# Sums and turns one to a slot at a block change, two stored pieces a step, x loaded in parts, the last block turned by TensorE, and a conversion that starts 6 half iterations later

## The chip, the cores and the metric

The kernel runs on one core of one Trainium2 chip. The metric is the device time of one execution in microseconds (us): 1709.61 us, the median of three runs (1707.02 to 1710.48). The profiled execution took 1710.2 us; its span, from the first instruction to the last, is 1708.4 us.

## The reference

Three layers follow one another, in float64 inputs and with a float32 result:

```python
p_packed = softmax_attention(p, k, v)          # 8 batches x 8 heads, 576 tokens, 32 packed queries, head 64
attn     = softmax_attention(q, p_packed, p_packed)
x        = attn as 4608 tokens x 512
h = x @ w_in                                   # 512 -> 2048
g = max(h, 0) + alpha * min(h, 0)
x = g @ w_out                                  # 2048 -> 512
g = x @ w_gate;  val = x @ w_val               # 512 -> 1536 each
out = (g / (1 + exp(-g)) * val) @ w_out2       # 1536 -> 512, returned as float32
```

## The kernel before, in words

All matmuls of the two large layers split their operands into a high and a low part and do three products for one (`mm3`: low weights by high x, high by high, high weights by low x).

The program has two phases. The first, 256 iterations, makes attention and the first large layer. Beside it, in half iterations (slots) from `GROUP0 = 84` on, DVE, ACT and POOL convert the weights of the last layer (`more_weights2`): each raw piece of 64-bit words becomes float32, is combined into seven forms, split in two and stored to device memory (`wgvd`, `wo2d`).

The second phase is the last layer, with a seven-product scheme for 2x2 blocks (forms A11, S2, A12, S3, S1, A22, S4). It goes over 6 blocks of 768 tokens and, in each, over 12 slices of the 1536 columns: 72 calls of `gv_step`, here called steps 0 to 71. One step does on PE seven products of six matmuls, into one bank of tag `h` (tiles xb, then vb) and one of tag `at` (yb). Each product but the first into a bank must wait until DVE or ACT has read what the product before left there: `u2 = yb + p1`, `u3 = yb + p1`, `u3 = vb + u3`, `p1 = yb + p1`, `u2 = vb + u2` on DVE (function `add`), p1 and the Silu on ACT. Between the products, at six places (`between(0)` to `between(5)`, called slots in this phase), stand the units of the output product of the step pair before: three matmuls each, seven units a step, so 63 matmuls a step.

The output of a block is summed in tiles `sums` (totals A12, S1, S2, A22, S4, each in two halves e = 0, 1) and in four banks o_acc that keep A11 and S3 over the whole block. When the last step pair of a block is done, which falls into the first two steps of the next block (steps 12 and 13, 24 and 25, ...), the totals are added to each other by `more`, turned by DVE's transpose into `os` or `osA` tiles by `put`, and stored by `store`, in four DMAs of 48 KB to a piece, eight pieces to a block. This is called a block change; there are five, and the sixth block ends the program in `out_last`.

SP's queue issues all loads: two tiles gv of a step's weights (`load_gv`, 896 KB each, two steps ahead, so that the buffers of step n take the weights of step n + 2), tiles wp of the output weights (`load_wo2`), and 16 DMAs a block that load the x of the next block into eight tiles xr (`load_x`). It also issues the stores, which `store` places behind the newest gv load.

The order of the work on each engine is set by a scheduler when the program is built; `tc.issue_after(ins)` keeps what is written in its block behind `ins` on the engine of `ins`. A wait on an engine holds everything behind it on that engine.

Of the kernel before, what the change touches and what calls it, by code (L numbers as in the profile page):

```python
# [108 lines left out]
def tile_kernel(  # L111
# [1031 lines left out]

    raw2, xs2, gvw, wo2 = {}, {}, {}, {}

    def load_x(s):
        for t in range(2):
            for c in range(KC):
# [62 lines left out]
    def prepare_x(s, name):  # L1211
        if name == "load":
            load_x(s)
        elif name == "S":
            sums_x(s)
        elif name == "D4":
            last_sum(s)
        else:
            split_x(s, name)
# [36 lines left out]
    def product(bank, n, k, start):  # L1256
# [14 lines left out]
                )  # L1271
        before[:] = [last]

    def add(out, bank, x):
        return nc.vector.tensor_tensor(out=out, in0=bank, in1=x, op=ALU.add)  # L1275

    def gv_step(n, between):

        s, f = divmod(n, NF2)
        p1, u2, u3, s1, s2 = (
            gp2.tile([P, T], F32, tag=t, name=f"{t}_{n}", bufs=b)
            for t, b in (("p1", 1), ("u2", 1), ("u3", 1), ("s1", 3), ("s2", 3))
        )
        def bank(tag, name):
            return ps.tile([P, 512], F32, tag=tag, name=f"{name}{n}", bufs=2)[:, :T]

# [36 lines left out]
        load_gv(n + 2)  # L1325
        store(n, 2)
# [11 lines left out]
    def form(m, name, x):  # L1338

        hi = gp2.tile([P, T], F32R, tag="fh", name=f"fh{m}_{name}", bufs=5)  # L1340
        nc.scalar.activation(out=hi, in_=x, func=AF.Copy)  # L1341
        lo = gp2.tile([P, T], F32R, tag="fl", name=f"fl{m}_{name}", bufs=5)
        by_dve = m == PAIRS - 1 and name in ("S2", "S4")
        (nc.vector if by_dve else nc.gpsimd).tensor_tensor(out=lo, in0=x, in1=f32(hi), op=ALU.subtract)  # L1344
        forms[m, name] = hi, lo

    def combine(out, x, y, op, last):
        engine = nc.vector if last else nc.gpsimd
# [21 lines left out]
    def forms_last(m):  # L1370

        last = m == PAIRS - 1
        a12, a22 = both[2 * m + 1]
        s2 = both[2 * m][0]
        form(m, "A22", a22)
        combine(a12, a12, s2, ALU.subtract, last)
        form(m, "S4", a12)

    banks, sums = {}, {}

# [14 lines left out]
                    sums[n, k] = tiles[j][:, c * T : (c + 1) * T]  # L1395
        return sums[name, e]

    def put(s, name, e, at_slot):

        t, dh = dict(A12=(0, 0), S4=(0, 1), A22=(1, 0), S1=(1, 1))[name]  # L1400
        if s == NBLK - 1:
            o = utile("u", [P, T], f"os{name}{e}_{s}")
        elif name == "A22":
# [6 lines left out]
        stores.append((at_slot, o, (2 * s + t) * T, 256 * dh + P * e))  # L1410
        if s == NBLK - 1:
            store(NBLK * NF2 + 9, 0)

    def store(n, i):

        for job in [j for j in stores if j[0] <= (n, i)]:
            stores.remove(job)
            at_slot, o, r0, c0 = job
            with tc.issue_after(newest[-1].ins) if n < NBLK * NF2 else ExitStack():
                for a in range(4):  # L1420
                    c = c0 + 32 * a
                    queue = nc.scalar if a % 2 and n > NBLK * NF2 else nc.sync
                    queue.dma_start(
                        out=out[r0 : r0 + T, c : c + 32].rearrange("(b j) i -> j b i", j=32),
                        in_=o[32 * a : 32 * a + 32].rearrange("p (b i) -> p b i", i=32),
                    )

    def more(to, e, x, engine=nc.vector):
        engine.tensor_tensor(out=total(to, e), in0=x, in1=total(to, e), op=ALU.add)  # L1429
# [9 lines left out]
            )  # L1439
        done(last)  # L1440

    def out_unit(m, i, at_slot):

        k, e = divmod(i, 2)
        name = OUT_FORMS[k]
# [11 lines left out]
        if first:  # L1457
            nc.scalar.activation(out=total(name, e), in_=bank, func=AF.Copy)
        else:
            more(name, e, bank)  # L1460
        if not last:
            return
        if name == "S1":
            more("S4", e, total("S1", e))
            more("S1", e, banks[f"acc{2 + e}"])
        elif name == "S2":
            u2 = total("S2", e)
            more("S1", e, u2)
            put(s, "S1", e, at_slot)
            more("A22", e, u2)  # L1470
            more("S4", e, u2, nc.gpsimd)
        else:
            put(s, name, e, at_slot)

    LAST = (
        ("A12", "A12"), ("S1", "S1"), ("S1", "S4"), ("S2", "S1"), ("S2", "A22"), ("A22", "A22"),
        ("S2", "S4"), ("S4", "S4"),
    )

    def out_last():  # L1480

        m = PAIRS - 1
        forms_later(m)
        forms_last(m)
        for e in range(2):
            more("S4", e, total("S1", e))
            more("S1", e, banks[f"acc{2 + e}"])
            for to in "S1", "A22", "S4":
                more(to, e, total("S2", e))
        at_end = {}  # L1490
        for tag, to in ("", "A12"), ("free", "S1"), ("acc0", "S4"), ("acc2", "A22"):
            for e in range(2):
                if tag == "free":
                    name = ("h", "at")[e]
                    at_end[to, e] = ps.tile([P, 512], F32, tag=name, name=f"oe{e}", bufs=2)[:, :T]
                else:
                    at_end[to, e] = banks[f"acc{int(tag[3:]) + e}" if tag else ("h", "at")[e]]
        for i, (name, to) in enumerate(LAST):
            start = to not in [t for _, t in LAST[:i]]
            stop = to not in [t for _, t in LAST[i + 1 :]]  # L1500
            for e in range(2):
                unit(at_end[to, e], m, OUT_FORMS.index(name), e, start, stop)
                if stop:
                    more(to, e, at_end[to, e])
                    put(NBLK - 1, to, e, (0, 0))

    due_at, after_at = {}, {}
    for m in range(PAIRS):
# [10 lines left out]
    def out_next(n, i):  # L1519

        for job in due_at.pop((n, i), ()):
            out_unit(*job, (n, i))
        if (n, i) in after_at:
            after_at.pop((n, i))()


    def steps(it, late):
# [27 lines left out]
    assert kinds[0] is None  # L1555
    gp1.close()
    gp2 = ctx.enter_context(tc.tile_pool(name="g2", bufs=1))
    for n in range(NBLK * NF2):
        gv_step(n, lambda i, n=n: out_next(n, i))
    assert not due_at and not after_at  # L1560
# [38 lines left out]
```

## Time and profile before

| | |
|---|---|
| median of three runs | 1709.61 us |
| profiled execution, its span | 1710.2 us, 1708.4 us |
| granted TensorE clock, mean | 0.968 |
| PE busy | 1590.0 us (93%), 10943 matmuls |
| DVE, POOL, ACT busy | 1098.1 us (64%), 1012.0 us (59%), 739.6 us (43%) |
| bytes moved by DMA | 330.74 MB |

Busy time is the sum over an engine's instructions; a clock of 1 is the higher of two levels, 2.4 GHz, and 0.5 the lower, 1.2 GHz. In rows of the timeline the first number is the start in us from the span's start, the second the time; `x4` are four instructions in a row, and the brackets hold the idle time of the engine before the row and what ended it. Matmuls are pipelined: one is listed with some 0.33 us, and the next starts 0.17 us after it.

### The profile page before, as it was taken

Reading aid. Unit: us, or ns where it says so; the run is one execution under the profiler, and the core shown is the slowest. Engines: PE = TensorE matmul, PEld = TensorE weight load, DVE = VectorE, ACT = ScalarE, POOL = GpSimd, SP = SyncE. Lnnn points to the kernel's source line nnn. Section 1 sums busy time; section 2 is a strip of 40 time slices with the busy share of each in tenths; the row PEclk is TensorE's granted clock in tenths of the full one; section 3 lists DMA queues with packets and bytes.
Section 4 is the critical chain, followed back from the end, with each engine's and each line's share of the span. In section 5 each row is a group of like instructions: output and inputs, shape, how many; then the busy total and the mean of one; then the engine's idle time right before and its main releaser. Section 6 shows DMA issues by size and latency. Waiting matters only on the chain.

```text
span 1708.4 us, 30336 instructions
## 1 busy us (share of the span) xinstructions
PE 1590.0 (93%) x10943; PEld 1493.3 (87%) x10943; DVE 1098.1 (64%) x1898; ACT 739.6 (43%) x1666; POOL 1012.0 (59%) x1063
## 2 busy tenths in 40 slices
PE   7598999989999999999999899989988998998897
PEld 4367798879898888989999899979988988998896
DVE  6868667575667676763356836845774683677357
ACT  6575654555555555555333333332322333233221
POOL 4748656666766767674456546655654664556552
PEclk8799999999999999999999999989999998999998
DMA  9414365646565555544666776776766687666762
GB/s 282 134 49 132 95 186 147 179 105 168 137 166 128 165 142 152 147 164 128 228 229 249 255 251 253 277 220 234 279 223 231 245 298 223 222 241 208 258 247 64
DMA packets 304231, 330.74 MB, mean 194 GB/s; under 512 B 206016, under 2 KB 257232, under 8 KB 299472
## 3 DMA queue, kind: packets, MB, share of 16 engines
q1 hardware_dynamic: 297680, 328.01, 59.9%
q8 instruction: 86, 1.41, 0.3%
q10 hardware_dynamic: 6400, 0.79, 0.3%
q14 instruction: 65, 0.53, 0.1%
HBM read 274.47 MB, written 54.26 MB: 192 GB/s over the span
## 4 chain that ended last, share of the span: by engine, by line
PE 70%; DVE 11%; DMA 6%; issue 4%; POOL 4%; ACT 2%; SPq 1%; DVEq 0%; POOLq 0%; ACTq 0%
PE acc L1115 6%; PE acc L1121 5%; PE acc L1116 5%; PE yb L326 4%; PE yb L328 4%; PE yb L327 4%; PE h L326 3%; DMA gv<-wgvd 3%; PE xb L326 3%; PE h L328 3%; PE h L327 3%; DVE sums L1429 3%; PE vb L326 3%; PE vb L327 3%; PE vb L328 3%
## 5 line engine op out<-in xcount | busy, mean ns | idle before, releaser
L1102 POOL TENSOR_TENSOR lo<-g,hi 128x288 fp32r<-128x288 f32 x256 | 233.1, 912 | 227.4 <-ACT hi L1100 187.3
L1092 DVE SCALAR_TENSOR_TENSOR g<-h,sg,m 128x288 f32<-128x288 f32 x256 | 130.6, 511 | 184.5 <-ACT m L1089 166.9
L1319 POOL TENSOR_TENSOR s<-s,u 128x384 f32<-128x384 f32 x72 | 73.0, 1013 | 256.3 <-ACT s L1312 256.3
L1275 DVE TENSOR_TENSOR u<-yb,p 128x384 f32<-128x384 f32 x144 | 80.0, 556 | 201.3 <-PE yb L328 185.6
L326 PE MATMUL h<-a2h,ppw 128*128 128x288 f32 x512 | 160.6, 314 | 31.7 <-DVE g L1092 22.6
L1349 POOL TENSOR_TENSOR s<-s,s 128x384 f32<-128x384 f32 x141 | 150.5, 1067 | 46.0 <-DVE s L1316 40.5
L1100 ACT ACTIVATE hi<-g 128x288 fp32r<-128x288 f32 x256 | 113.0, 442 | 144.8 <-DVE g L1092 141.7
L326 PE MATMUL yb<-ring,gv 128*128 128x384 f32 x432 | 149.9, 347 | 21.7 <-DVE u L1275 21.7
L1344 POOL TENSOR_TENSOR fl_S<-s,fh_S 128x384 fp32r<-128x384 f32 x142 | 145.4, 1032 | 25.4 <-ACT fh_S L1341 25.1
L1089 ACT ACTIVATE m<-h,sal 128x288 f32<-128x288 f32 x256 | 126.3, 495 | 66.3 <-PE h L328 65.4
L328 PE MATMUL h<-a2l,ppw 128*128 128x288 f32 x512 | 152.5, 299 | 2.2 <-POOL a2l L562 2.1
L326 PEld LDWEIGHTS h<-a2h,ppw 128*128 128x128 f32 x512 | 97.3, 190 | 63.8 <-DVE g L1092 33.2
L327 PE MATMUL h<-a2h,ppw 128*128 128x288 f32 x512 | 152.2, 297 | 0.0
L327 PE MATMUL yb<-ring,gv 128*128 128x384 f32 x432 | 147.8, 342 | 0.0
L328 PE MATMUL yb<-ring,gv 128*128 128x384 f32 x432 | 147.7, 342 | 0.0
L1275 DVE TENSOR_TENSOR u<-vb,u 128x384 f32<-128x384 f32 x144 | 79.9, 555 | 92.3 <-PE vb L328 92.3
L1312 ACT ACTIVATE s<-p 128x384 f32<-128x384 f32 x72 | 37.8, 525 | 213.4 <-DVE p L1275 213.4
L1344 POOL TENSOR_TENSOR fl_A<-s,fh_A 128x384 fp32r<-128x384 f32 x108 | 112.5, 1042 | 27.1 <-ACT fh_A L1341 26.0
L326 PE MATMUL xb<-ring,gv 128*128 128x384 f32 x288 | 101.1, 351 | 25.9 <-DMA gv<-wgvd 21.9
L326 PEld LDWEIGHTS yb<-ring,gv 128*128 128x128 f32 x432 | 83.7, 194 | 26.1 <-DVE u L1275 26.1
L985 POOL TENSOR_TENSOR cva<-cva,cva 128x256 fp32r<-128x256 f32 x126 | 96.9, 778 | 10.2 <-ACT cva L984 9.6
L328 PEld LDWEIGHTS h<-a2l,ppw 128*128 128x128 f32 x512 | 97.4, 191 | 4.6 <-POOL a2l L562 3.8
(297 smaller groups left out, 5027.8 us busy)
## 6 DMA issues: line engine op xcount, KB each, us to landing
gv<-wgvd SPq DMA_DIRECT2D x144, 896.0 KB, 8.0
wp<-wo2d SPq DMA_DIRECT2D x36, 1024.0 KB, 5.1
wp<-wo2d SPq DMA_DIRECT2D x36, 768.0 KB, 4.4
wgvd<-cva SPq DMA_DIRECT2D x84, 256.0 KB, 2.8
wo2d<-cva SPq DMA_DIRECT2D x42, 256.0 KB, 2.6
v<-in_v_dram SPq DMA_DIRECT2D x16, 576.0 KB, 4.8
cva<-in_moe_w_in_dram SPq DMA_DIRECT2D x7, 1024.0 KB, 8.8
kr<-in_k_dram SPq DMA_DIRECT2D x96, 72.0 KB, 2.7
```

Of the source, the lines that this page charges most:

```text
L326: nc.tensor.matmul(o, wlo, xhi, start=start, stop=False, **kw)
L327: nc.tensor.matmul(o, whi, xhi, start=False, stop=False, **kw)
L328: return nc.tensor.matmul(o, whi, xlo, start=False, stop=stop, **kw)
L985: nc.gpsimd.tensor_tensor(out=lo, in0=full, in1=f32(hi), op=ALU.subtract)
L1089: begun[it] = marks[f"u{it}"] = nc.scalar.activation(out=m, in_=hp, func=AF.Copy, scale=sal[:, f : f + 1])
L1092: made[it] = marks[f"m{it}"] = nc.vector.scalar_tensor_tensor(out=g32, in0=hp, scalar=sg[:, f : f + 1], in1=m, op0=ALU.mult, op1=ALU.max)
L1100: rounded[n] = nc.scalar.activation(out=hi, in_=x, func=AF.Copy)
L1102: nc.gpsimd.tensor_tensor(out=lo, in0=x, in1=f32(hi), op=ALU.subtract)
L1115: nc.tensor.matmul(acc[dc], lo[:, f % WP, c], ghi, start=start, stop=False)
L1275: return nc.vector.tensor_tensor(out=out, in0=bank, in1=x, op=ALU.add)
L1344: (nc.vector if by_dve else nc.gpsimd).tensor_tensor(out=lo, in0=x, in1=f32(hi), op=ALU.subtract)
L1349: engine.tensor_tensor(out=out, in0=x, in1=y, op=op)
```

## The change

- `NEXT_X`: the x of the next block is no longer loaded by one call at slice 3, but by four calls at slices 2 to 5 (x00, x10, x12, x02), two tiles each.
- `later`, `do_later`: at a block change, the additions of totals to each other and the turns are put into a list, `jobs2`, and `out_next` takes one of them at each slot, behind the newest `add`. The two additions S4 += S2 stay on POOL at once.
- `store` stores two pieces at the end of a step, whatever is ready.
- `sums_ahead`, `out_last`: in the last block S4 += S1 goes to POOL at step 71; the other additions of totals stand behind `forms_last`. The totals are turned by PE (three 128x128 transposes against `ident` to a piece), copied by ACT and stored in one DMA a piece, where before DVE turned them and four DMAs on SP and ACT stored a piece.
- `GROUP0`: 90 for 84.

```diff
-GROUP0 = 84
+GROUP0 = 90
-NEXT_X = dict(load=3, A11=6, S=6, S2=7, A12=8, D4=9)
+NEXT_X = dict(x00=2, x10=3, x12=4, x02=5, A11=6, S=6, S2=7, A12=8, D4=9)
...
     def add(out, bank, x):
-        return nc.vector.tensor_tensor(out=out, in0=bank, in1=x, op=ALU.add)
+        ins = nc.vector.tensor_tensor(out=out, in0=bank, in1=x, op=ALU.add)
+        ahead[:] = [ins]
+        return ins
...
+    def store():
+        for _ in range(min(len(stores), 2)):
+            o, r0, c0 = stores.pop(0)
+            with tc.issue_after(newest[-1].ins):
...
+    def do_later():
+        if jobs2:
+            with tc.issue_after(ahead[-1].ins):
+                jobs2.pop(0)[2]()
...
-        if name == "S1":
-            more("S4", e, total("S1", e))
-            more("S1", e, banks[f"acc{2 + e}"])
+        if name == "A12":
+            wait.append(("A12", e, lambda: put(s, "A12", e)))
+        elif name == "S1":
+            later("S1", e, lambda: more("S4", e, total("S1", e)))
+            later("S1", e, lambda: more("S1", e, banks[f"acc{2 + e}"]))
...
         elif name == "S2":
-            u2 = total("S2", e)
-            more("S1", e, u2)
-            put(s, "S1", e, at_slot)
-            more("A22", e, u2)
-            more("S4", e, u2, nc.gpsimd)
+            more("S4", e, total("S2", e), nc.gpsimd)
+            if e:
+                for i in range(2):
+                    later("S2", i, lambda i=i: more("S1", i, total("S2", i)))
...
+    LAST = """
+        A12-A12 S1-S1 S1-S4 combined >A120 >A121 S2-S1 S2-A22 A22-A22 >S10 >S11 S2-S4 S4-S4
+        >A220 >A221 >S40 >S41
+    """
...
+                for g in range(T // P):
+                    c = slice(g * P, (g + 1) * P)
+                    last = nc.tensor.transpose(bank[:, c], total(to, e)[:, c], ident)
...
+            nc.scalar.activation(out=o, in_=bank, func=AF.Copy)
+            nc.sync.dma_start(
```

DVE at the first block change, from the read of vb that ends step 12 to the first read of yb in step 13 (u2_13), before:

```order
L1275 TENSOR_TENSOR u2_12_12090<-vb12_12152,u2_12_12090 128x384
L1429 TENSOR_TENSOR sums0_10977<-o_acc2_10922,sums0_10977 128x384
L1429 TENSOR_TENSOR sums0_10977<-o_h_10973,sums0_10977 128x384
L1429 TENSOR_TENSOR sums0_10977<-o_acc3_10951,sums0_10977 128x384
L1429 TENSOR_TENSOR sums1_10978<-o_at_10989,sums1_10978 128x384
L1316 TENSOR_TENSOR s1_12_12092<-s1_12_12092,u2_12_12090 128x384
L1429 TENSOR_TENSOR sums0_10977<-sums0_10977 128x384
L1429 TENSOR_TENSOR sums1_10978<-sums0_10977,sums1_10978 128x384
L1429 TENSOR_TENSOR sums0_10977<-sums1_10978,sums0_10977 128x384
L1429 TENSOR_TENSOR sums1_10978<-sums1_10978 128x384
L1275 TENSOR_TENSOR u2_13_12230<-yb13_12235,p1_13_12229 128x384
```

The same stretch now, and on to the second read of yb (u3_13):

```order
L1279 TENSOR_TENSOR u2_12_12090<-vb12_12149,u2_12_12090 128x384
L1444 TENSOR_TENSOR sums0_10977<-o_acc2_10922,sums0_10977 128x384
L1444 TENSOR_TENSOR sums0_10977<-o_h_10973,sums0_10977 128x384
L1322 TENSOR_TENSOR s1_12_12092<-s1_12_12092,u2_12_12090 128x384
L1444 TENSOR_TENSOR sums1_10978<-o_at_10989,sums1_10978 128x384
L1279 TENSOR_TENSOR u2_13_12212<-yb13_12217,p1_13_12211 128x384
L1444 TENSOR_TENSOR sums1_10978<-o_h_10973,sums1_10978 128x384
L1444 TENSOR_TENSOR sums1_10978<-sums0_10977,sums1_10978 128x384
L1444 TENSOR_TENSOR sums0_10977<-o_acc3_10951,sums0_10977 128x384
L1279 TENSOR_TENSOR u3_13_12213<-yb13_12217,p1_13_12211 128x384
```

The four additions of totals to totals have left the place ahead of u2_13; one of them stands behind it, and three follow in the rest of step 13 and in step 14.

SP at the first block change, from the gv load that step 13 issues for step 15 to the next but one, before (gv15 belongs to step 15; os and osA are stores):

```order
L1236 DMA gv15_0_12332<-wgvd3_484 128x1792
L1236 DMA gv15_1_12333<-wgvd3_484 128x1792
L1423 DMA out_0_dram<-os_12136 32x12x32 x8
L1423 DMA out_0_dram<-osA220_0_12254 32x12x32 x4
L1423 DMA out_0_dram<-osA221_0_12274 32x12x32 x4
L1423 DMA out_0_dram<-os_12136 32x12x32 x4
L1245 DMA wp8_0_12438<-wo2d2_495 128x2048
L1236 DMA gv16_0_12468<-wgvd4_485 128x1792
L1236 DMA gv16_1_12469<-wgvd4_485 128x1792
L1423 DMA out_0_dram<-os_12136 32x12x32 x4
```

The same stretch now:

```order
L1238 DMA gv15_0_12315<-wgvd3_484 128x1792
L1238 DMA gv15_1_12316<-wgvd3_484 128x1792
L1429 DMA out_0_dram<-os_12255 32x12x32 x8
L1247 DMA wp8_0_12412<-wo2d2_495 128x2048
L1238 DMA gv16_0_12447<-wgvd4_485 128x1792
L1238 DMA gv16_1_12448<-wgvd4_485 128x1792
L1429 DMA out_0_dram<-os_12255 32x12x32 x8
L1247 DMA wp8_1_12532<-wo2d2_495 128x1536
L1238 DMA gv17_0_12563<-wgvd5_486 128x1792
```

Twenty stores stood between two steps' gv loads, and now eight do, as they do behind the gv loads of the two steps that follow.

SP in steps 10 and 11, where the x of block 2 is loaded, now (before, the same sixteen DMAs stood at the same two places, with tiles 02 and 03 ahead of 10 to 13):

```order
L1155 DMA xr2_00_12459<-x1d5_80 128x192
L1155 DMA xr2_00_12459<-x1d6_81 128x192
L1155 DMA xr2_01_12462<-x1d5_80 128x192
L1155 DMA xr2_01_12462<-x1d6_81 128x192
L1247 DMA wp6_0_11933<-wo2d0_493 128x2048
L1238 DMA gv12_0_11963<-wgvd0_481 128x1792
L1238 DMA gv12_1_11964<-wgvd0_481 128x1792
L1155 DMA xr2_10_12575<-x1d6_81 128x96
L1155 DMA xr2_10_12575<-x1d7_82 128x288
L1155 DMA xr2_11_12578<-x1d6_81 128x96
```

The scheduler places the four calls of slices 2 to 5 of block 1 into steps 10 and 11, around the same gv load as before.

## Rows read from the trace of the kernel before

**Rows 1.** Waits of PE: who waited for whom, us in total, times, longest
```profile
PE xb L326 <- DMA gv<-wgvd: 21.9, 5, 5.2
PE yb L326 <- DVE u L1275: 21.7, 10, 4.1
```

**Rows 2.** Timeline of PE at the first block change, steps 13 and 16
```profile
961.79 0.44 PE L326 MATMUL xb<-ring,gv 128*128 128x384 f32 x1 [0.50 <-DVE u L1275]
...
965.38 0.34 PE L328 MATMUL xb<-ring,gv 128*128 128x384 f32 x1
969.79 0.44 PE L326 MATMUL yb<-ring,gv 128*128 128x384 f32 x1 [4.08 <-DVE u L1275]
...
1004.46 0.66 PE L326 MATMUL xb<-ring,gv 128*128 128x384 f32 x1 [3.59 <-DMA gv<-wgvd]
```

**Rows 3.** Stretches: length, busy us (x) of PE, PEld, DVE, ACT, POOL, clock, DMA share
```profile
961.80:1017.00 55.20, 47.53 (x252) 46.92 (x253) 28.64 (x47) 16.72 (x36) 29.28 (x28) 0.94 0.71 225
1107.00:1163.60 56.60, 48.53 (x253) 47.92 (x254) 28.76 (x47) 16.72 (x36) 29.27 (x28) 0.91 0.68 220
1253.60:1312.30 58.70, 49.78 (x252) 49.17 (x253) 28.65 (x47) 16.72 (x36) 29.25 (x28) 0.88 0.67 212
1402.40:1459.90 57.50, 48.23 (x253) 47.62 (x254) 28.65 (x47) 16.72 (x36) 29.27 (x28) 0.91 0.68 216
1549.90:1607.10 57.20, 48.87 (x252) 48.25 (x253) 28.66 (x47) 16.71 (x36) 29.28 (x28) 0.91 0.69 217
1618.10:1672.90 54.80, 54.80 (x316) 54.80 (x316) 29.82 (x55) 16.16 (x34) 34.51 (x35) 1.00 0.67 243
```

**Rows 4.** Timeline of DVE at the first block change
```profile
959.71 1.56 DVE L1429 TENSOR_TENSOR sums<-sums,sums 128x384 f32<-128x384 f32 x2
961.19 0.55 DVE L1275 TENSOR_TENSOR u<-vb,u 128x384 f32<-128x384 f32 x1
...
964.10 1.37 DVE L1429 TENSOR_TENSOR sums<-sums 128x384 f32<-128x384 f32 x1
965.39 2.62 DVE L1429 TENSOR_TENSOR sums<-sums,sums 128x384 f32<-128x384 f32 x2
967.93 1.34 DVE L1429 TENSOR_TENSOR sums<-sums 128x384 f32<-128x384 f32 x1
969.19 0.55 DVE L1275 TENSOR_TENSOR u<-yb,p 128x384 f32<-128x384 f32 x1
```

**Rows 5.** Timeline of POOL beside these
```profile
965.01 1.31 POOL L1349 TENSOR_TENSOR s<-s,s 128x384 f32<-128x384 f32 x1
```

**Rows 6.** Timeline of SP's queue, steps 12 to 15; the time is that of the issue
```profile
959.92 0.79 SPq L1236 DMA_DIRECT2D gv<-wgvd  x2
...
978.48 9.15 SPq L1423 DMA_DIRECT2D out_dram<-os  x8
987.73 4.00 SPq L1423 DMA_DIRECT2D out_dram<-osA  x8
...
994.38 1.81 SPq L1236 DMA_DIRECT2D gv<-wgvd  x2
```

**Rows 7.** The page's DMA issues: count, KB each, us from issue to landing
```profile
gv<-wgvd SPq DMA_DIRECT2D x144, 896.0 KB, 8.0
```

**Rows 8.** Timeline at the end: PE, DVE, and SP's last stores
```profile
1687.92 0.69 PE L326 MATMUL o_h<-fh_A,wp 128*128 128x384 f32 x1 [3.33 <-ACT fh_A L1341]
...
1684.91 1.94 DVE L1429 TENSOR_TENSOR sums<-o_acc,sums 128x384 f32<-128x384 f32 x4
...
1701.15 1.01 DVE L1409 STREAM_TRANSPOSE osS<-sums 128x384 f32<-128x384 f32 x2
...
1702.87 2.14 SPq L1423 DMA_DIRECT2D out_dram<-osS  x4
```

**Rows 9.** One line's instructions: the phase-one transposes by PE, ns min/median/max
```profile
L704 PE MATMUL et<-ident,E x72: 270/272/275, 218.1 to 684.7; 128*96 128x128 f32 x72
```

**Rows 10.** Timeline of PE in iteration 233 of phase one
```profile
762.91 0.40 PE L326 MATMUL h<-a2h,ppw 128*128 128x288 f32 x1 [2.34 <-DVE g L1092]
```

More of the change, by code (lines that the diff above doesn't have):

```diff
@@ L1144, in tile_kernel, with load_x @@
     raw2, xs2, gvw, wo2 = {}, {}, {}, {}
-    def load_x(s):
-        for t in range(2):
-            for c in range(KC):
+    def load_x(s, ts=range(2), cs=range(KC)):
+        for t in ts:
+            for c in cs:
                 raw = utile("u", [P, T], f"xr{s}_{t}{c}")
@@ L1213, in prepare_x @@
             load_x(s)
+        elif name[0] == "x":
+            load_x(s, (int(name[1]),), range(int(name[2]), int(name[2]) + 2))
         elif name == "S":
@@ L1325, in gv_step @@
         load_gv(n + 2)
-        store(n, 2)
+        store()
         if s + 1 < NBLK:
@@ L1343, in form @@
         by_dve = m == PAIRS - 1 and name in ("S2", "S4")
-        (nc.vector if by_dve else nc.gpsimd).tensor_tensor(out=lo, in0=x, in1=f32(hi), op=ALU.subtract)
         forms[m, name] = hi, lo
+        return (nc.vector if by_dve else nc.gpsimd).tensor_tensor(
+            out=lo, in0=x, in1=f32(hi), op=ALU.subtract
+        )
     def combine(out, x, y, op, last):
@@ L1396, in total, with place, put @@
         return sums[name, e]
-    def put(s, name, e, at_slot):
+    def place(s, name, e):
         t, dh = dict(A12=(0, 0), S4=(0, 1), A22=(1, 0), S1=(1, 1))[name]
-        if s == NBLK - 1:
-            o = utile("u", [P, T], f"os{name}{e}_{s}")
-        elif name == "A22":
+        return (2 * s + t) * T, 256 * dh + P * e
+    def put(s, name, e):
+        if name == "A22":
             o = utile("x", [P, T], f"os{name}{e}_{s}")
@@ L1409, in put @@
         nc.vector.transpose(out=o, in_=total(name, e))
[L1410 to L1419, printed above, removed]
+        stores.append((o, *place(s, name, e)))
+    def store():
+        for _ in range(min(len(stores), 2)):
+            o, r0, c0 = stores.pop(0)
+            with tc.issue_after(newest[-1].ins):
                 for a in range(4):
                     c = c0 + 32 * a
-                    queue = nc.scalar if a % 2 and n > NBLK * NF2 else nc.sync
-                    queue.dma_start(
+                    nc.sync.dma_start(
                         out=out[r0 : r0 + T, c : c + 32].rearrange("(b j) i -> j b i", j=32),
@@ L1426, in store, with later @@
                     )
+    def later(name, e, fn):
+        jobs2.append((name, e, fn))
+    def do_later():
+        if jobs2:
+            with tc.issue_after(ahead[-1].ins):
+                jobs2.pop(0)[2]()
     def more(to, e, x, engine=nc.vector):
@@ L1457, in out_unit @@
         if first:
+            assert not [j for j in jobs2 if j[:2] == (name, e)]
             nc.scalar.activation(out=total(name, e), in_=bank, func=AF.Copy)
@@ L1462, in out_unit, with sums_ahead @@
             return
-        if name == "S1":
-            more("S4", e, total("S1", e))
-            more("S1", e, banks[f"acc{2 + e}"])
-        elif name == "S2":
-            u2 = total("S2", e)
-            more("S1", e, u2)
-            put(s, "S1", e, at_slot)
-            more("A22", e, u2)
-            more("S4", e, u2, nc.gpsimd)
-        else:
[L1473 to L1478, printed above, removed]
+        if name == "A12":
[4 more added lines that the diff above has]
+            if e:
+                jobs2.extend(wait)
+                wait.clear()
+        elif name == "S2":
+            more("S4", e, total("S2", e), nc.gpsimd)
+            if e:
+                for i in range(2):
+                    later("S2", i, lambda i=i: more("S1", i, total("S2", i)))
+                for i in range(2):
+                    later("S1", i, lambda i=i: put(s, "S1", i))
+                for i in range(2):
+                    later("S2", i, lambda i=i: more("A22", i, total("S2", i)))
+        else:
+            later(name, e, lambda: put(s, name, e))
+    wait = []
+    LAST = """
+        A12-A12 S1-S1 S1-S4 combined >A120 >A121 S2-S1 S2-A22 A22-A22 >S10 >S11 S2-S4 S4-S4
+        >A220 >A221 >S40 >S41
+    """
+    def sums_ahead():
+        for e in range(2):
+            more("S4", e, total("S1", e), nc.gpsimd)
     def out_last():
@@ L1483, in out_last @@
         forms_later(m)
-        forms_last(m)
+        after = forms_last(m)
+        to_bank = {}
         for e in range(2):
-            more("S4", e, total("S1", e))
-            more("S1", e, banks[f"acc{2 + e}"])
-            for to in "S1", "A22", "S4":
[L1489 to L1505, printed above, removed]
+            to_bank["A12", e] = banks[("h", "at")[e]]
+            to_bank["S1", e] = ps.tile(
+                [P, 512], F32, tag=("h", "at")[e], name=f"oe{e}", bufs=2
+            )[:, :T]
@@ new lines, in out_last, with turned @@
+            to_bank["S4", e] = banks[f"acc{e}"]
+            to_bank["A22", e] = banks[f"acc{2 + e}"]
+        def turned(to, e):
+            bank = to_bank[to, e]
+            with behind():
+                for g in range(T // P):
+                    c = slice(g * P, (g + 1) * P)
+                    last = nc.tensor.transpose(bank[:, c], total(to, e)[:, c], ident)
+            done(last)
+            o = utile("u", [P, T], f"os{to}{e}")
+            nc.scalar.activation(out=o, in_=bank, func=AF.Copy)
+            r0, c0 = place(NBLK - 1, to, e)
+            nc.sync.dma_start(
+                out=out[r0 : r0 + T, c0 : c0 + P].rearrange("(g p) d -> p g d", p=P),
+                in_=o.rearrange("p (g d) -> p g d", d=P),
+            )
@@ new lines, in combined @@
+        def combined():
+            for e in range(2):
+                more("S1", e, banks[f"acc{2 + e}"])
+            for to in "S1", "A22", "S4":
+                for e in range(2):
+                    more(to, e, total("S2", e))
+        with tc.issue_after(after.ins):
+            for word in LAST.split():
+                if word == "combined":
+                    combined()
+                    continue
+                if word[0] == ">":
+                    turned(word[1:-1], int(word[-1]))
+                    continue
+                name, to = word.split("-")
+                for e in range(2):
+                    left = [w for w in LAST.split() if w.endswith("-" + to)]
+                    unit(
+                        to_bank[to, e], m, OUT_FORMS.index(name), e, word == left[0],
+                        word == left[-1],
+                    )
+                    if word == left[-1]:
+                        more(to, e, to_bank[to, e])
```

9 lines of the change are left out of this document (6 added, 3 removed).

## The prediction

> **What bounds the kernel now.** I read the waits first, then the timeline of PE at the places that they name, then stretches that compare these places with quiet ones. PE is busy for 93% of the span, so only time in which PE stands still or runs at the lower clock is to be had. Two waits of PE stand out in the second phase [rows 1]: 21.9 us for gv, five times, up to 5.2 us, and 21.7 us for DVE's u, ten times, up to 4.1. The reader is to see that five is the number of block changes. At the first [rows 2], step 13 waits 4.08 us for DVE before its second product into yb, and step 16 waits 3.59 us for its weights. The other short waits for u lie elsewhere and are left alone.
>
> The stretches size it [rows 3]. Five steps without a change take 54.80 us at clock 1.00, so 10.96 us a step. The four steps from 13 to 16 of each change take 55.2, 56.6, 58.7, 57.5 and 57.2 us, together 285.2, where 20 quiet steps take 219.2. The excess is 66.0 us. Of it 20.4 is the wait for DVE (5 x 4.08, with 4.1 the longest) and 21.9 the wait for gv, together 42.3. The rest, 23.7, is the lower clock: the granted means 0.94, 0.91, 0.88, 0.91 and 0.91 times the lengths lack 3.3 + 5.1 + 7.0 + 5.2 + 5.1 = 25.7 us of full clock. After each long wait part of the next matmuls runs at the lower of the two levels, as the first ones after the waits show (0.44 and 0.66 us listed, against 0.33 in a quiet step). Without the waits this goes too.
>
> **The change part by part.** *Sums one to a slot.* Why does DVE come late? [rows 4] Between the read of vb at 961.19 and u at 969.19 stand nine instructions, and the last four, which add totals to totals, take 5.1 us (964.10 to 969.19). PE wanted u at about 965.6, behind its last matmul into xb (965.38 [rows 2]). In the order now, four instructions stand between the two reads: three additions from banks (0.48 us each, as four take 1.94 [rows 8]) and the product s1 (0.6, an estimate near the 0.55 of a row alone). From 961.7 that is 963.7. PE's yb, whose 12 matmuls start at 961.79 and follow at 0.17, is done near 964.0, so u starts when yb is there and ends at 964.6, 1.0 us ahead of need. The 4.08 us go.
>
> The additions come back behind it. In step 13 I count on DVE, with its five reads of xb, vb and yb, the additions from banks and two turns, 13 instructions at about 0.48, three additions of totals at 1.3 and the product s1 at 0.9 (between 0.55 and 1.3): 11.0 us in a step of 10.96. So DVE is full for one step, and not over it; step 14 has about 8. PE leaves DVE 1.0 us (the two units after the last product of a step) to 2.1 us (two units and a product) for each read. The trace has one such case: at 959.71 two additions of totals stand ahead of the read of vb and PE waits 0.50 us [rows 2, 4]. These two stand there still. What is new I bound from that wait below, if it went too (5 x 0.50 = 2.5 us gained), and above by four additions of 1.3 us a change, each wholly on PE's path (5 x 4 x 1.3 = 26 us). The nearest row is the 0.50 wait, so I take one more of it at each change: 2.5 us lost.
>
> By the Trainium skill's page "SBUF — State Buffer", section "Who interferes with whom", a VectorE instruction with both inputs in SBUF and a GpSimd instruction that reads SBUF exclude each other, and the loser waits for the whole of the other. The trace agrees: beside POOL instructions of 1.31 us [rows 5] the additions take 1.34 to 1.37 us [rows 4]. By this rule spreading them makes none of them cheaper, since POOL is busy for more than half of these steps; what that can cost is worked out from rows as the first rival.
>
> *Two stored pieces a step.* Before, SP issued 20 stores between the gv loads of step 15 and of step 16: 9.15 us for eight behind the gv transfers, 4.00 for the next eight, 2.0 for four, and the gv load came at 994.38 [rows 6]. A gv pair is issued near a step's end (959.92, where step 13 begins at 961.79 after 0.50 of wait [rows 2, 6]), so it is needed 1.4 + 10.96 = 12.4 us after its issue, and lands after 8.0 (median) [rows 7]: a margin of about 4 us, against which twenty stores spend 15.2, more than a step. Now eight stores follow each of four gv pairs. That costs SP 9.15 + 0.79 us [rows 6] and a wp load of about 0.8 with its waits (an estimate from the 0.79 of a gv pair), 10.7 in a step of 10.96: no step's load is late by more than some tenths, and the margin takes these. So the 21.9 us go. The DMA engines have the room: their share is 0.67 in quiet steps [rows 3].
>
> *x in parts.* The order shows the sixteen loads in steps 10 and 11, as before, around the same gv load. This part moves nothing: 0, within 1 us either way.
>
> *The last block.* Before, PE waits 3.33 us for the rounded A12, since DVE adds four banks (1.94 us) ahead of the product s1 that makes it [rows 8]. Now two of these and an addition of totals are gone from there, so PE goes on about 1.7 us earlier. After the wait PE runs at the lower clock (0.69 us listed [rows 8]); a wait half as long may not bring that, and I take 1.5 us for it, between 0 and 2.5 (16 matmuls at 0.32 for 0.17). Against this PE turns pieces: 24 transposes at 0.11 us (the spacing of rows that list 0.27 each [rows 9]), of which 18 stand among the matmuls, 2.0 us; and the turns of A12 stand ahead of 30 matmuls and wait for DVE, about 1 us. So PE ends about as before, 0.2 us earlier. Behind it, from DVE's last turns at 1701.15 to the end at 1708.4, went 7.2 us: two turns of 1.01, stores issued until 1705.0, their landing [rows 8]. Now come six transposes with their start (0.7), two copies (1.0), one DMA (0.4 in place of 2.14 us of issuing) and the same 3.4 behind the last issue: 5.5, less 1.1 since the first of the two pieces runs ahead: 4.4. Gain 2.8 + 0.2 = 3.0 us. Bounds: 6 us (the whole wait of 3.33 and the 2.8), and a loss of 1 (PE stays at the lower clock, and DVE's ten additions hold the turns of A12 for 4 us).
>
> *Conversion 6 slots later.* In the order DVE's conversion leaves iterations 228 to 230, where it stood among the work on x and PE waited 2.34 us [rows 10]; it also leaves 67 and 68. From iteration 91 on the order by attention block is mostly the same, shifted by one iteration in places, and may open short waits there. Gain 2.0, bounds 5 gained and 4 lost.
>
> Sum, against the profiled execution's own 1710.2 us (span 1708.4, 1.8 around it; 0.6 above the median of the runs): 1710.2 - 66.0 + 2.5 - 3.0 - 2.0 = 1641.7 us.
>
> **The rivals.** *The additions still hold PE.* POOL's instructions of 1.31 us stretch DVE's additions of totals to 1.34 and more [rows 4, 5]. If four of them a change each meet such an instruction just before a read that PE waits for, each costs 1.1 us beyond the slack: 5 x 4 x 1.1 = 22, so 1664. For it: DVE at 11.0 us in step 13. Against: at 959.71 two such additions cost only 0.50. The page named above speaks for it.
>
> *The weights still come late.* The x loads have not moved, and SP is nearly full for four steps in a row. If each step's lateness adds up past the margin, the 21.9 us and their half of the lower clock, 11.8, remain: 1641.7 + 33.7 = 1675. For it: 10.7 us on SP against 10.96, so little is left. Against: to use up 4 us in four steps, each would have to take 12 us.
>
> *Slower: the turns of S4 wait for the stores of A12.* Both use the same two places of `os`, and A12 is now stored a step later, at the end of step 13; S4 is turned at the end of step 14. If the store's landing slips by a step, DVE stands at that turn for 11 us with all reads behind it, PE stands for 10 and loses some 3 us to the lower clock. From 13.7 us a change (68.5 / 5) it decides the sign; with a slip of one and a half steps, 16.5 us, the time is 1641.7 + 82.5 = 1724. For it: the place that is shared. Against: eight stores were issued within 9.15 us [rows 6], and the turn comes about 12 us after the gv pair ahead of them.
>
> *No change* needs the two waits to be replaced by others of the same size; nothing in the rows speaks for it.
>
> **How the numbers follow.** The forecast, 1641.7, has 0.66, with its own range 1633 (the bounds of the gains at the end and in phase one, and the 0.50 waits gone) to 1652 (both as losses). The additions 0.18 (1652 to 1668), the weights 0.10 (1675), no change 0.02, slower 0.04. A range of 1631 to 1665 holds the first and most of the second. A measurement can tell 0.2%, 3.4 us, from no change: faster 0.94, same 0.02, slower 0.04.
>
> **What would show it.** Right: the waits of PE no longer name gv at xb, and u at yb only with short ones; the stretches of steps 13 to 16 come near 44.4 us at clock 1.00; SP shows stores in four groups of eight with a gv pair between; DVE is busy for nearly all of step 13; the last store is issued within 3 us of PE's last matmul. Wrong: PE idle for more than 1 us in steps 13 or 14 behind a `sums` row of DVE (first rival), gv issued later in each of steps 14 to 17 (second), DVE idle before a turn of S4 with a store's landing as what ended it (third). If the time falls by far less than 66 us while these waits are gone, the lower clock has another cause than the waits.

## The result and the profile after

The changed kernel takes 1647.6 us (median of 4 runs, 1644.56 to 1649.89) against 1708.96 (4 runs, 1707.02 to 1710.48): a ratio of 0.964, 95% interval 0.9621 to 0.966. Forecast were 1641.7 us, with a range of 1631 to 1665. The profiled execution took 1648.21 us; its span is 1646.3.

The windows cut both spans at the same two places: the first matmul into xb, and the start of step 71. The columns are those of [rows 3]; the last is GB/s. Before:

```profile
0.00:822.70 822.70, 764.24 (x6390) 679.66 (x6391) 547.45 (x928) 461.04 (x1067) 515.62 (x580) 0.97 0.53 149
822.70:1672.90 850.20, 802.58 (x4441) 791.73 (x4441) 524.65 (x922) 273.65 (x590) 489.05 (x476) 0.97 0.69 243
1672.90:1708.40 35.50, 23.16 (x116) 21.95 (x114) 25.99 (x50) 4.95 (x10) 7.30 (x7) 0.84 0.28 45
```

After:

```profile
0.00:830.50 830.50, 767.35 (x6390) 682.21 (x6391) 549.95 (x928) 455.89 (x1067) 514.83 (x580) 0.97 0.52 148
830.50:1614.60 784.10, 780.90 (x4442) 771.38 (x4442) 515.73 (x922) 273.93 (x590) 491.23 (x477) 1.00 0.76 263
1614.60:1646.30 31.70, 24.76 (x139) 23.48 (x137) 20.24 (x40) 8.42 (x18) 9.19 (x9) 0.94 0.18 50
```

The second phase is 66.1 us shorter, at full clock throughout; the last step and what follows it, 3.8 shorter; the first phase is 7.8 *longer*, with PE busy for 3.1 us more and idle for the rest.

**Block changes.** The waits of PE, as in [rows 1]:

```profile
PE h L326 <- DVE g L1092: 24.5, 17, 5.3
...
PE yb L326 <- DVE u L1279: 1.4, 5, 0.3
...
PE xb L326 <- DMA gv<-wgvd: 0.2, 1, 0.2
```

Of gv's 21.9 us one wait of 0.2 is left, at step 30, behind the second block change, and of u's 21.7 us five waits of 0.3. The largest is now in the first phase. Steps 13 to 16, to set beside [rows 3], at the first change (44.2 us at clock 1.00 at each of the others too):

```profile
969.20:1013.40 44.20, 44.20 (x253) 43.90 (x254) 28.22 (x50) 16.73 (x36) 29.54 (x28) 1.00 0.86 274
```

Five times 44.2 are 221.0, where 285.2 stood: 64.2 less, with 1.8 above twenty quiet steps. Some 0.5 us a change came in front of these stretches, since the wait of 0.50 at the start of step 13 [rows 2] shrank too.

DVE at the first change, to be read beside [rows 4], and two of POOL's rows that lie in it:

```profile
971.55 0.56 DVE L1279 TENSOR_TENSOR u<-yb,p 128x384 f32<-128x384 f32 x1 [0.65 <-PE yb L328]
...
973.29 1.35 DVE L1444 TENSOR_TENSOR sums<-sums,sums 128x384 f32<-128x384 f32 x1 [0.72 <-POOL sums L1444]
...
978.41 0.53 DVE L1444 TENSOR_TENSOR sums<-sums 128x384 f32<-128x384 f32 x1
...
973.22 1.01 POOL L1351 TENSOR_TENSOR fl_A<-s,fh_A 128x384 fp32r<-128x384 f32 x1
...
979.12 1.01 POOL L1325 TENSOR_TENSOR s<-s,u 128x384 f32<-128x384 f32 x1 [3.60 <-ACT s L1318]
```

u now waits for PE (0.65 us), where PE waited 4.08 for u. By the Trainium skill's page "SBUF — State Buffer", section "Who interferes with whom", a VectorE instruction with two inputs in SBUF contends with a GpSimd instruction that reads SBUF. The rows agree: an addition of totals takes 1.35 us beside POOL's 973.22, and 0.53 at 978.41, in the 3.60 us for which POOL stood idle. No read was late by it.

SP's queue, to set beside [rows 6]:

```profile
979.19 0.80 SPq L1238 DMA_DIRECT2D gv<-wgvd  x2
980.04 9.74 SPq L1429 DMA_DIRECT2D out_dram<-os  x8
...
990.40 0.85 SPq L1238 DMA_DIRECT2D gv<-wgvd  x2
991.34 10.13 SPq L1429 DMA_DIRECT2D out_dram<-os  x8
...
1002.08 0.85 SPq L1238 DMA_DIRECT2D gv<-wgvd  x2
1003.02 8.18 SPq L1429 DMA_DIRECT2D out_dram<-osA  x8
...
1012.12 0.82 SPq L1238 DMA_DIRECT2D gv<-wgvd  x2
```

Four groups of eight, as forecast (the fourth follows the last pair shown). From gv pair to gv pair it is 11.2, 11.7 and 10.0 us, and 12.0 behind the fourth group (10.7 forecast). The tightest pair of this change, issued at 990.40, landed at 1000.69 for a step that began at 1002.34: 1.65 us of the margin are left. At the second change nothing was left once:

```profile
1146.40 0.85 SPq L1238 DMA_DIRECT2D gv<-wgvd  x2
1147.34 11.40 SPq L1429 DMA_DIRECT2D out_dram<-os  x8
...
1159.36 1.00 SPq L1238 DMA_DIRECT2D gv<-wgvd  x2
```

Here 13.0 us lie between the pairs. The first of them took 11.9 us to land, and PE waited 0.2 for it at 1158.40.

**The end**, beside [rows 8]:

```profile
1627.70 0.44 PE L326 MATMUL o_h<-fh_A,wp 128*128 128x384 f32 x1 [1.49 <-ACT fh_A L1347]
1628.95 0.69 PE L328 MATMUL o_h<-fl_A,wp 128*128 128x384 f32 x1 [0.63 <-POOL fl_A L1351]
```

The wait for fh_A fell by 1.84 us (1.7 forecast); a wait of 0.63 for POOL is new. The lower clock came behind these shorter waits too, as the 0.69 of the second row shows, but for less time: from step 71 on 0.94 was granted, where it was 0.84.

**The first phase.** Its windows from iteration 62 to 101, to 197 (three batches of attention), to 229 and to the end, before and after:

```profile
271.30:388.50 117.20, 110.34 (x964) 100.09 (x957) 76.11 (x132) 61.79 (x149) 74.54 (x91) 0.99 0.58 159
388.50:660.80 272.30, 266.96 (x2445) 245.12 (x2443) 182.67 (x318) 154.16 (x369) 178.59 (x214) 0.99 0.55 147
660.80:750.80 90.00, 88.53 (x817) 81.25 (x816) 61.90 (x107) 52.00 (x125) 59.40 (x71) 1.00 0.57 169
750.80:822.70 71.90, 69.56 (x524) 69.28 (x524) 30.62 (x54) 34.24 (x78) 35.82 (x42) 1.00 0.40 137
```

```profile
271.20:384.20 113.00, 108.61 (x964) 99.83 (x957) 74.86 (x130) 60.80 (x147) 71.90 (x87) 0.98 0.58 155
384.20:665.10 280.90, 269.88 (x2444) 246.68 (x2443) 184.27 (x318) 150.91 (x369) 178.24 (x214) 0.99 0.54 145
665.10:760.20 95.10, 91.19 (x816) 83.50 (x815) 62.31 (x107) 51.11 (x125) 59.46 (x72) 0.96 0.55 160
760.20:830.50 70.30, 69.87 (x525) 69.40 (x524) 32.86 (x58) 35.56 (x83) 41.88 (x49) 1.00 0.46 156
```

The two ends gained 4.2 and 1.6 us; the middle lost 8.6 and 5.1. Of the 8.6, 5.7 are idle time of PE (11.0 in place of 5.3 us) and 2.9 longer busy time.

Among the waits of ACT for a DMA between 384 and 665 us, w_val's load has 2.3 us before, and stores of wo2d 0.3; after, these two lead:

```profile
ACT cva L244 <- DMA cva<-in_moe_w_val_dram: 12.1, 4, 4.4
ACT cva L984 <- DMA wo2d<-cva: 10.9, 3, 4.6
```

One place of the first row, after, on POOL, SP, ACT and PE:

```profile
458.25 1.31 POOL L287 TENSOR_TENSOR cva<-cva 128x512 f32<-128x512 f32 x1
...
451.70 9.83 SPq L618 DMA_DIRECT2D kr<-in_k_dram  x13
461.63 0.58 SPq L968 DMA_DIRECT2D cva<-in_moe_w_val_dram  x1
...
466.84 0.66 ACT L244 ACTIVATE cva<-cva 128x512 f32<-128x512 f32 x1 [4.35 <-DMA cva<-in_moe_w_val_dram]
...
473.48 0.40 PE L326 MATMUL h<-a2h,ppw 128*128 128x288 f32 x1 [1.74 <-DVE g L1092]
```

POOL frees the raw tile at 459.56, but SP issues thirteen k loads until 461.53. The raw load goes out 2.0 us late, ACT stands for 4.35, and DVE's g, behind the work that piled up, holds PE within the next 7 us. That became the theory (C): the later start puts w_val's load behind the k loads. It leaves out the second row, the wait for stores of wo2d, which SP issues too; e6 bears on that.

### The profile page after: what moved, and what is told of

The parts are those of the page before. It is cut to its first block, busy times and chain, and to the rows that moved or that the text cites. A ratio compares the mean times of both kernels' runs of the same rounds, so it can differ in the third digit from the quotient of the medians.

```text
span 1646.3 us, 30365 instructions
## 1 busy us (share of the span) xinstructions
PE 1573.0 (96%) x10967; PEld 1477.1 (90%) x10967; DVE 1085.9 (66%) x1888; ACT 738.2 (45%) x1674; POOL 1015.3 (62%) x1065
## 4 chain that ended last, share of the span: by engine, by line
PE 66%; DVE 11%; issue 7%; DMA 6%; POOL 5%; ACT 4%; SPq 0%; DVEq 0%; POOLq 0%; ACTq 0%
PE yb L326 4%; PE acc L1115 4%; PE yb L328 4%; PE yb L327 4%; PE acc L1116 4%; PE acc L1121 4%; PE xb L326 3%; PE vb L327 3%; PE vb L326 3%; PE vb L328 3%; PE xb L327 3%; PE xb L328 3%; PE h L326 2%; DMA cva<-in_moe_w_val_dram 2%; PE h L328 2%
## 5 line engine op out<-in xcount | busy, mean ns | idle before, releaser
L326 PE MATMUL yb<-ring,gv 128*128 128x384 f32 x432 | 145.5, 337 | 1.4 <-DVE u L1279 1.4
L328 PE MATMUL yb<-ring,gv 128*128 128x384 f32 x432 | 144.4, 334 | 0.0
L327 PE MATMUL yb<-ring,gv 128*128 128x384 f32 x432 | 144.4, 334 | 0.0
L1347 ACT ACTIVATE fh_S<-s 128x384 fp32r<-128x384 f32 x144 | 72.7, 518 | 69.9 <-POOL s L1357 67.1
```

The costliest lines, as they stand in the source:

```text
L326: nc.tensor.matmul(o, wlo, xhi, start=start, stop=False, **kw)
L327: nc.tensor.matmul(o, whi, xhi, start=False, stop=False, **kw)
L328: return nc.tensor.matmul(o, whi, xlo, start=False, stop=stop, **kw)
```

## The experiments

Each ran beside the kernel before on the same chip (medians 1708.5 to 1710.2). Times of the first phase come from one execution each: in six programs that order it alike (the changed kernel, e3, e4, e5, e7 and e9) it took 825.5 to 830.5 us.

**e1, the start alone undone.**

```diff
-GROUP0 = 90
+GROUP0 = 84
```

> The changed kernel with one part undone: the conversion starts at slot 84 again. Theory C (the later start costs the 7.8 us by which the second phase of the changed kernel begins later, 830.5 against 822.7 us, since a raw load of an attention period now stands behind sixteen loads of k on SP and ACT waits 3 to 5.5 us for it): the second phase starts near 822.7 again and the time falls by about 7.8, to 1640. Rival N (the first phase varies by so much from one build to another, whatever the start): about 1647.6, within 3. The prediction's own step (the later start gains 2.0): 1649.6.

Measured: 1638.35 us (ratio 0.9579, 0.956 to 0.9598). First phase 824.7; iterations 101 to 197:

```profile
389.10:661.50 272.40, 267.13 (x2445) 245.15 (x2443) 182.54 (x318) 153.80 (x369) 178.36 (x213) 0.99 0.54 147
```

That is theory C's number for these batches; the whole time fell by 9.2 us, where 7.8 were expected. The k loads stand here ahead of a load of w_out, which ACT uses 3 us after it has landed:

```profile
449.95 11.41 SPq L618 DMA_DIRECT2D kr<-in_k_dram  x16
462.49 0.34 SPq L968 DMA_DIRECT2D cva<-in_moe_w_out_dram  x1
```

**e2, the kernel before with the start alone at 90** (the same line, 84 to 90).

> The kernel before with one part alone: the conversion starts at slot 90. Theory C: slower by the same 7.8 us, 1709 + 7.8 = about 1717 (ratio 1.0045), with the second phase starting near 830.5. Rival N: about 1709. The prediction's step: 1707.

Measured: 1716.28 us, ratio 1.0037 (1.0022 to 1.0053), first phase 832.6. That step alone makes the kernel slower, by 6.7 us of the medians, where e1 gave 9.2. Against e1 and the kernel before (824.7 and 822.7), the first phases of the seven programs at 90 average 829.3 us: in these single executions the start costs some 5.6 us, and the 7.8 of the one pair holds some scatter. The three batches are clear of it: 277.3 to 280.9 us in the seven programs, 272.3 and 272.4 at 84. Rival N falls.

**e3, sums and turns at once.**

```diff
-        jobs2.append((name, e, fn))
+        fn()
```

(and A12's turn goes through the same function)

> The changed kernel with all sums and turns of a block change issued at once again, in the places on DVE that they had before; two stored pieces a step, x in parts, the last block and the start at 90 stay. Theory W (the wait of PE for u2 at step 13 is one of two separate waits, and the lower clock goes with it): 20.4 us of waits come back, and 11.4 of the 23.7 us that the lower clock cost (its share of 42.3 us of waits), so 1647.6 + 31.8 = 1679; PE waits for gv stay away. Rival G (the stores alone were the trouble, the sums are hidden when SP is in time): below 1655. Rival L (nearly all of the 23.7 us belong to this wait): 1692.

Measured: 1678.92 us (0.9818, 0.9799 to 0.9837). The second phase, and PE at the first change:

```profile
829.70:1644.10 814.40, 788.76 (x4443) 779.22 (x4442) 524.57 (x922) 273.69 (x590) 489.88 (x477) 0.99 0.73 254
```

```profile
976.79 0.44 PE L326 MATMUL yb<-ring,gv 128*128 128x384 f32 x1 [4.08 <-DVE u L1279]
```

The wait returns to the hundredth, and waits for gv stay away. The phase is 30.3 us longer: 22.8 of waits for u (21.7 + 2.5 against 1.4), 7.5 of lower clock. Theory W holds, with more of waits and less of the clock than it counted (20.4 and 11.4); G and L fall.

**e4, x loaded by one call.**

```diff
-NEXT_X = dict(x00=2, x10=3, x12=4, x02=5, A11=6, S=6, S2=7, A12=8, D4=9)
+NEXT_X = dict(load=3, A11=6, S=6, S2=7, A12=8, D4=9)
```

> The changed kernel with x of the next block loaded by one call at slice 3 instead of four calls at slices 2 to 5. The prediction's step: no change, 1647.6 within 1. Rival: sixteen loads at once hold the gv load of their step, 5 times up to 3 us: up to 1662.

Measured: 1644.74 us (0.9621, 0.9599 to 0.9644). The second phase takes 783.5 us against 784.1: nothing, as forecast. The first phase, which this edit does not touch, was 5 us shorter in that execution: the scatter named above.

**e5, all ready pieces stored; e9, three pieces a step.**

```diff
-        for _ in range(min(len(stores), 2)):
+        for _ in range(len(stores)):
```

> The changed kernel with all ready pieces stored at the end of a step: 12, 16 and 4 DMAs behind three gv pairs in place of four times eight. Theory S (what counts is how many stores stand between two gv pairs; before, twenty cost 4.4 us of PE's wait on average): four stores fewer at 0.5 us leave 2.4 us a change, with the lower clock in the same proportion as before (66.0 to 42.3) 5 x 2.4 x 1.56 = 19, so 1666. Rival M (the margin of 4 us between gv's landing and its use takes sixteen stores): 1648.

> The changed kernel with three stored pieces a step: 12, 12 and 8 DMAs behind three gv pairs. Theory A (lateness on SP adds up from step to step, up to the margin of 4 us): 9.15 + 4 x 0.5 + 1.6 = 12.8 us in a step of 10.96, late by 1.8 and then 3.7, within the margin: PE waits less than 0.5 us a change, 1648 to 1651. Rival T (each step with more than eight stores costs its own lateness, whatever the margin): 5 x 3.7 x 1.56 = 29, 1676.

Measured: e5 1669.35 us (0.9768, 0.9741 to 0.9794), e9 (3 in place of 2) 1658.31 (0.9712, 0.9689 to 0.9734). Second phases 807.4 and 795.2 us, 23.3 and 11.1 longer. The wait for gv, in e5 and in e9:

```profile
PE xb L326 <- DMA gv<-wgvd: 15.9, 7, 3.1
```

```profile
PE xb L326 <- DMA gv<-wgvd: 7.5, 9, 1.5
```

SP in e9, from the second group of twelve on:

```profile
991.47 0.97 SPq L1238 DMA_DIRECT2D gv<-wgvd  x2
992.53 5.69 SPq L1429 DMA_DIRECT2D out_dram<-os  x4
998.33 6.22 SPq L1429 DMA_DIRECT2D out_dram<-osA  x8
...
1005.16 0.85 SPq L1238 DMA_DIRECT2D gv<-wgvd  x2
```

Lateness adds up, as theory A has it: step 16's weights land 0.14 us before use, step 17 waits 1.18. But the price counted was too low: the second twelve took 11.9 us (13.7 from pair to pair, where 12.8 was counted), and the pair for step 16 took 10.2 us to land (10.3 in the changed kernel), where a median of 8 was counted. The margin there was 1.65 us, not 4, and gone after one step. So A fell in size and T in kind. e5 came near theory S's 1666, with 15.9 us of waits where S counted 12; M falls. Eight stores a step is the largest of the counts tried that costs next to nothing (the one wait of 0.2 us).

**e7, the old end.** All of `out_last` as before, of which:

```diff
+        nc.vector.transpose(out=o, in_=total(name, e))
...
+        for a in range(4):
...
-            nc.scalar.activation(out=o, in_=bank, func=AF.Copy)
```

> The changed kernel with the end of the kernel before: all additions of totals in their old places, DVE turns, four stores a piece. The stretch from the last step's start to the span's end was 35.5 us before and 31.7 after; theory: this comes back whole, 3.8 us, so 1651.4. The prediction's own step: 3.0, so 1650.6. Rival: the gain came from S4's earlier addition alone (POOL at step 71), so less than 2 come back.

Measured: 1649.76 us (0.9647, 0.9625 to 0.967). The whole time tells little here, but the stretch does: from step 71 it is 35.5 us again, and PE waits 3.34 for fh_A:

```profile
1627.48 0.44 PE L326 MATMUL o_h<-fh_A,wp 128*128 128x384 f32 x1 [3.34 <-ACT fh_A L1347]
```

So the 3.8 us belong to the end as a whole; the rival, less than 2, falls.

**e6, the raw loads on another queue, start at 90.**

```diff
-            nc.sync.dma_start(out=like(spots["raw"], src), in_=src)
+            nc.scalar.dma_start(out=like(spots["raw"], src), in_=src)
```

(in the second run `nc.gpsimd`, POOL, in place of `nc.scalar`)

> The changed kernel (start at 90) with the raw loads of the converted weights issued by ACT instead of SP; all else as it is. Theory Q (the later start is dear because in each attention period a raw load stands behind sixteen loads of k on SP, so ACT's widening waits 3 to 5.5 us for it): the second phase starts 5 to 8 us earlier than 830.5, and the time is about 1641. Rival P (the loads come in time, and the loss comes from the conversion's instructions on ACT, DVE and POOL that now meet other work of the attention): 1648, within 3. ACT's own issuing of 36 loads of 0.4 us may cost some of the gain.

> The same with the raw loads issued by POOL, whose own subtraction is what frees the raw buffer. Theory Q: about 1641, as on ACT, unless issuing on POOL costs more than the 0.4 us of SP. Rival P: 1648. If ACT and POOL differ, the queue that issues has a price of its own.

Measured: by ACT 1631.18 us (0.9537, 0.9518 to 0.9556), by POOL 1646.01 (0.9626, 0.9604 to 0.9648). By ACT the load of the place shown above leaves at 454.15, as soon as POOL has freed the tile (at 454.12, where SP let 2.0 us pass), and ACT waits 1.62 for it; the three batches take 271.8 us:

```profile
459.73 0.67 ACT L244 ACTIVATE cva<-cva 128x512 f32<-128x512 f32 x1 [1.62 <-DMA cva<-in_moe_w_val_dram]
```

In these batches theory Q has its gain (9.1 us). The other 7.6 of the first phase's 16.7 lie outside them and are not explained by it. On POOL an issue of this load takes twice the time of one on SP or ACT (0.39 and 0.38, medians), and as busy time of the engine:

```profile
L968 POOL DMA_DIRECT2D cva<-in_moe_w_val_dram x12: 766/770/776, 239.4 to 741.8; - x12
```

ACT then waits for w_val eleven times, 23.6 us in all from 250 to 820 us (24.6 in the changed kernel), and nothing is gained that the runs can tell. The three batches take 280.9 us as before the move, although ACT's wait for stores of wo2d fell there from 10.9 to 2.8 us: that speaks against this wait as what makes them long, though POOL's longer issues came in beside it. The page "DMA: Bandwidth & Descriptors" of the Trainium skill, section "Rules for kernel authors", says that spreading DMAs over issuing engines brings no bandwidth and saves only issue time on the sequencer; ACT's run agrees, with the DMA share at 0.55 in these batches, where it was 0.54.

**e8 and e10, raw loads on ACT with the start at 84 and at 96; e11, on SP with the start at 96.**

> The changed kernel with the raw loads on ACT and the conversion started at 84 again. Theory Q (the start matters only through the place of the raw loads on SP): with ACT issuing, 84 and 90 are equal, 1631 within 3, and the second phase starts near 813.8. Rival R (the two gains are separate things): 1631.2 less the 9.3 that the start gave with SP, 1622.

> As above with the start at 96, six slots later still. Theory Q: 1631 within 3. Rival R (a later start costs by itself, 9 us for six slots): 1640. The last conversion may by then reach into the end of the first phase.

> The changed kernel, raw loads on SP as there, the conversion started at 96. Theory V (what costs is which raw load falls behind the run of k loads on SP: w_val, which ACT uses at once, at the start 90, but w_out at 84 and w_gate at 96, which are used 2.4 to 5 us after they land): iterations 101 to 197, 280.9 us in the changed kernel and 272.4 at 84, take about 272 again, and the time is about 1638. Rival R (a later start costs by itself, about 1.5 us a slot): 1657. Rival J (the start has no part in it, the programs differ by chance): 1648.

Measured: e8 1645.23 us (0.9629, 0.9615 to 0.9642), e10 1629.92 (0.9538, 0.9525 to 0.9551), e11 1626.15 (0.9513, 0.9499 to 0.9527). The three batches take 269.0 us in e10; in e8 and in e11:

```profile
385.90:662.60 276.70, 269.39 (x2445) 246.72 (x2443) 182.38 (x318) 151.93 (x369) 178.85 (x214) 0.99 0.55 149
```

```profile
378.40:645.40 267.00, 265.69 (x2444) 243.63 (x2443) 180.36 (x318) 154.67 (x369) 176.49 (x214) 1.00 0.56 152
```

e8 refutes Q as it stood: off SP, 84 and 90 differ by 14 us, 4.9 of them in the three batches. An issue on ACT that waits for POOL to free the raw tile holds ACT instead, as this wait of e8 between 384 and 665 us shows:

```profile
ACT m L1089 <- POOL cva L287: 7.0, 4, 2.0
```

It has no counterpart with the loads on SP; but it stands in e6 too (9.5 us), so it does not tell the two starts apart. R falls with both starts: later is not dearer. e11 bears out V's direction (w_gate behind the k loads, w_val clear of them) and shows that V is not the whole: 267.0 us where 272 was expected, and 1626 in all where V gave 1638. J falls.

e11 is faster than both kernels, 1.3% below the changed one. Open stays why 96 beats 84 by 12 us, and why the order by start is 84, 96 ahead of 90 on SP but 90, 96 ahead of 84 on ACT. Of the 18.5 us by which e11's first phase is shorter than e1's (806.2 us), 5.4 lie in the three batches and 9.2 in the iterations 62 to 101 ahead of them (108.2 against 117.4). The runs show that the start decides, by up to 21 us, and for one place (w_val behind the k loads at 90) through which queue. That it acts through the place of the conversion within an attention batch is argued for the rest, not shown: no run shifted the start by a whole batch.

## Why the prediction was right, and where not

- *Sums one to a slot, weights in time, lower clock: 66.0 us.* With the new waits in it (63.5 forecast) the second phase measured 66.1. e3 and e5 take the two causes apart: sums at once cost 30.3 us, stores at once 23.3, and both together 66.1. The 12.5 left over belong to the pair: at once the sums make five pieces ready for one step (twenty stores), spread out four (sixteen). Some 6 of them are waits for gv (21.9 us with both causes, 15.9 in e5), the rest the lower clock. One reading was wrong without harm to the sum: a row of 0.44 us does not show the lower clock, since it is listed after the wait of 0.50 too [rows 2], with rows of 0.33 and 0.34 behind it. Rows of 0.52, 0.32 apart, show it; after the wait of 4.08 they begin at 970.32.
- *New waits behind additions: 2.5 us lost.* They were there, but smaller, and an old one shrank: 1.8 us in steps 13 to 16 (0.2 at 977.14 of the first change, where PE's unit waits for DVE's addition from o_at, is the clearest), against 2.4 less in the five steps 12. Near zero in all, inside the bounds. Rival one needed reads without slack. DVE was to be full in step 13 (11.0 us); it was busy for 9.8, since additions away from POOL take 0.55.
- *Two stored pieces a step: right, but with nothing to spare.* A step's load took up to 11.7 us on SP in the groups shown for the first change and 13.0 at the second, for 10.7. A quiet step issues its pair 9.8 us after it starts; at the changes that was up to 1.0 us later (first) and 2.5 (second), not some tenths. The lateness did not add up past the margin, so rival two did not occur as it was put. But the margin was smaller than 4 us, since the pairs took 8.4 to 11.9 us to land at the changes, where the median of 8.0 was counted: 1.65 us were left at the first change and none at step 30. With twelve stores none is left. That the 21.9 us went but for 0.2 was in part luck.
- *The turns of S4 never waited for stores*: no wait of DVE names a store or stands ahead of a turn. Rival three does not occur.
- *x in parts: 0*, borne out by e4. *The end: 3.0, measured 3.8*, borne out by e7. What follows PE's last unit is 2.8 us shorter, as counted; that unit starts at 1699.13 before and 1639.84 now, 1.0 us earlier in the stretch, where 0.2 was counted.
- *The step that failed: "Conversion 6 slots later ... Gain 2.0, bounds 5 gained and 4 lost."* In the profiled pair it lost 7.8 us, and 5.6 by the averages under e2. A gain at the two ends, where [rows 10] lie, was there: 4.2 and 1.6 us, the first not clear of the scatter (113.0 to 117.9 us over the seven programs at 90, 117.2 before). But I called the order between "mostly the same, shifted by one iteration in places" and bounded it with 4, where nearly two hundred iterations hold some six batches: 8.6 us lost in three, 5.1 in the one behind them. What I did not do was to follow the moved DMAs past SP's other loads, as I had for the stores. The error of the sum, 5.9 us, is this term (9.8) less 2.6 and 0.8 from the two others that came out better, and 0.6 of the profiled execution. The forecast's own low end was mis-added: with the waits of 0.50 gone the term of 2.5 lost becomes 2.5 gained, 5.0 and not 2.5, and the end 1631 and not 1633.

## What to carry to other kernels

A shift by a few slots of background work that recurs with the same period as the foreground can be paid once per period: multiply by the number of periods before you bound it, and look at each queue for what the moved loads now stand behind. Where several transfers share a queue with a deadline, count the time between two deadlines (here 10.97 us) and let the rest wait; lateness adds up from step to step. Sweep such a start before anything cleverer: six slots one way were worth 9 us, six the other way 21.

## What the runs showed of the hardware

- What eight stores behind a gv pair cost SP ends, all but the last two, with the landing of the pair. In each of the changed kernel's twenty groups the sixth store's issue ended 0.1 to 0.8 us before the pair had landed. Two or three of the fourth to sixth issues took 1.2 to 3.9 us each; the seventh and eighth took 0.3 to 1.4, mostly 0.47. Behind the pair that landed at 1000.69 the fourth took 3.55 us, the last two 0.48 and 0.47. Four stores more therefore cost only some 1.9 us (e9: 12.8 and 13.7 us from pair to pair at the first change, where it was 11.2 and 11.7), but a pair that lands late makes the next one late.
- After each wait of 4.08 us for DVE in e3, the lower clock cost some 1.5 us (7.5 over five changes); in the kernel before, with two long waits three steps apart, 66.1 less the 44.6 of waits that went, 4.3 a change.
